# Loading chunks 1 to 3 of x from a second DMA queue in a transformer-block kernel

## The chip, the cores and the metric

The kernel runs on one core of a Trainium2 chip. The metric is the device time of one execution in microseconds (us), of the slowest core, which here is the only one. The kernel before takes 799.41 us (median of 3 runs, 799.39 to 799.5).

Engines carry their short names in the profile: PE is TensorE (PEld its weight loads), DVE is VectorE, ACT is ScalarE, POOL is GpSimd, SP is SyncE. SPq and ACTq are the sequencers of SyncE and ScalarE, which issue DMAs. Times in the views count from the start of the profiled span.

## The reference

A pre-norm block: a segmented attention with a memory, then a gated MLP, both with a residual. Only its first step matters here: the layer norm of x, 2048 rows of 1024 in bf16, and the projection of its first 512 rows.

```python
def _layernorm(x, axis=-1, eps=1e-05):
    m = jnp.mean(x, axis=axis, keepdims=True)
    v = jnp.var(x, axis=axis, keepdims=True)
    return (x - m) / jnp.sqrt(v + eps)

x = A_x
h = x + _A_ref(_layernorm(x, axis=-1), A_wq, A_wk, A_wv, A_wo, A_beta)   # attention, 4 segments of 512
h2 = h + _B_ref(_layernorm(h, axis=-1), B_w_in, B_w_sp, B_b_sp, B_w_out) # gated MLP
```

## The kernel before

A small recorder lists the operations of each engine in program order and puts in the semaphore waits. (So every operation has the same source line, L209, in the profile.) Each engine has its own instruction stream; SyncE does nothing but issue DMAs.

The first segment is four chunks of 128 rows of x, 256 KB each. They are loaded in turn with four 256 KB pieces of w_v, all by SyncE:

```python
def x_load(tc):
    sp.dma_start(XCH[tc % 4][:], x2d[tc * 128:(tc + 1) * 128, :])

for k in range(8):
    if k in (0, 1, 3, 5):
        x_load((k + 1) // 2)
    else:
        i = {2: 0, 4: 2, 6: 4, 7: 6}[k]
        sp.dma_start(WV[0][:, i:i + 2, :],
                     A_wv[i * 128:(i + 2) * 128, 0:512].rearrange("(c p) n -> p c n", p=128))
sp.dma_start(WK[:, :, 0:256], wcols(A_wk, 0, 256))
sp.dma_start(BETAB[:], A_beta.partition_broadcast(128))
# ... more weights ...
act.activation(RDM[:, 0, 0:1], MHALF[:], ACTF.Exp)   # ScalarE's first activation: brings its table load forward
```

The start of the computation. `warm` keeps TensorE busy while x is under way; `center` subtracts the mean (the division comes later, in the projections); `pe_Th` transposes a chunk on TensorE with eight 128-wide matmuls and copies the result out:

```python
warm(9)                                    # nine 512-wide matmuls on zeros
act_mean(1)                                # mean of chunk 1 on ScalarE
var0(ln_stats(XCH[0]))                     # mean and variance of chunk 0 on VectorE
c0 = center(0, MV[0][:, 0:1], ALU.subtract)
c1 = center(1, MEAN[1][:])
pe_Th(0, c0, dve, dve)
pe_Th(1, c1, act, dve)
act_mean(2)
rstd0(0)
var0(ln_stats(XCH[1]))
rstd0(1)
c2 = center(2, MEAN[2][:])
act_mean(3)
# ... first half of the w_v projection of chunks 0 and 1, then pe_Th(2, c2, act, dve) ...
```

The softmax here doesn't subtract the row's maximum and nothing guards it: scores larger than these inputs give would overflow.

Of the kernel before, what the change touches and what calls it, by code (L numbers as in the profile page):

```python
# [257 lines left out]
def bass_sequential_preLN__memory_aug_infini_attn__mixer_gmlp__prompt_kernel(  # L258
# [14 lines left out]
    x2d = A_x[0]  # L273
    out2d = out[0]
    R = _Recorder(nc)
    pe, act, dve, pool, sp = R.pe, R.act, R.dve, R.pool, R.sp
# [69 lines left out]
    XCH = [b2("xch%d" % i, [128, D], BF16) for i in range(4)]  # L346
# [43 lines left out]
            pe.matmul(dst, lhs(i), rhs(i), start=(i == 0), stop=(i == n - 1))  # L390


    def x_load(tc):
        sp.dma_start(XCH[tc % 4][:], x2d[tc * 128:(tc + 1) * 128, :])

    def wcols(ap, lo, hi):
        return ap[:, lo:hi].rearrange("(c p) n -> p c n", p=128)

    for k in range(8):
        if k in (0, 1, 3, 5):  # L400
            x_load((k + 1) // 2)
        else:
            i = {2: 0, 4: 2, 6: 4, 7: 6}[k]
            sp.dma_start(WV[0][:, i:i + 2, :],
                         A_wv[i * 128:(i + 2) * 128, 0:512].rearrange("(c p) n -> p c n", p=128))
# [318 lines left out]
    for tc in range(4, 8):  # L724
        x_load(tc)
# [44 lines left out]
    for n in range(LAST + 1):  # L770
# [30 lines left out]
        if s < NSEG - 2 and c >= 4:  # L801
            x_load(4 * (s + 2) + c - 4)
# [87 lines left out]
    for tb in range(4):  # L890
# [9 lines left out]
        for tcl in range(4):  # L900
            tc = 4 * tb + tcl
# [38 lines left out]
```

## Time and profile before

| | kernel before |
|---|---|
| time, median of 3 | 799.41 us |
| traced run | 799.35 us |
| TensorE busy | 790.4 of 797.3 us |
| chunk 0 asked for / landed | 0.80 / 3.54 us |
| first transpose starts | 5.80 us |
| transposes of chunk 2 start | 9.97 us |

The page of the kernel before, its busy times and the chain that ended last:

```profile
PE 790.4 (99%) x5657; PEld 378.9 (48%) x5657; DVE 377.3 (47%) x745; ACT 295.5 (37%) x347; POOL 170.6 (21%) x329
...
PE 96%; DVE 2%; ACT 1%; issue 0%; DMA 0%; DVEq 0%
```

TensorE is the limit. A change of the first DMAs can only matter where TensorE stands still for want of their data, which is in the first 10 us. There, the chain of waits of the kernel before, in order of time (start, length, what):

```profile
0.80 2.74 DMA xch<-in_A_x_dram
...
3.56 0.70 DVE stats L209
...
5.26 0.50 DVE lno L209
...
5.80 1.74 PE ps L209 x16
...
7.57 0.42 DVE xnT L209
...
9.57 0.36 DVE lno L209
...
9.97 13.08 PE ps L209 x80
```

Read it from below: the long run of TensorE that begins at 9.97 us waits for chunk 2 to be centred on VectorE. VectorE goes from one thing to the next since the statistics of chunk 0, with two short waits for the transposes (0.31 and 0.27 us), and the statistics wait for the DMA of chunk 0. That is the only DMA on the chain.

The timeline of the same run (start, length, engine, operation, tiles, count; in brackets the idle time before and what ended it):

```profile
0.79 1.28 ACT L209 ACT_TABLE_LOAD   x1 [0.79 <-PEq L925]
0.80 0.87 SPq L209 DMA_DIRECT2D xch<-in_A_x_dram  x2
...
4.25 1.06 ACT L209 ACTIVATE junk<-xch 128x1024 bf16<-128x1024 bf16 x1 [1.96 <-DMA xch<-in_A_x_dram]
...
5.80 1.73 PE L209 MATMUL ps<-ident,lno 128*128 128x128 bf16 x16 [0.18 <-DVE lno L209]
```

ScalarE does wait for chunk 1, but its mean is done before VectorE asks for it. The sixteen transposes take 1.73 us.

### The profile page before, as it was taken

Reading aid. Unit: us, or ns where it says so; the run is one execution under the profiler, and the core shown is the slowest. Engines: PE = TensorE matmul, PEld = TensorE weight load, DVE = VectorE, ACT = ScalarE, POOL = GpSimd, SP = SyncE. Lnnn points to the kernel's source line nnn. Section 1 sums busy time; section 2 is a strip of 40 time slices with the busy share of each in tenths; the row PEclk is TensorE's granted clock in tenths of the full one; section 3 lists DMA queues with packets and bytes.
Section 4 is the critical chain, followed back from the end, with each engine's and each line's share of the span. In section 5 each row is a group of like instructions: output and inputs, shape, how many; then the busy total and the mean of one; then the engine's idle time right before and its main releaser. Section 6 shows DMA issues by size and latency. Waiting matters only on the chain.

```text
span 797.3 us, 13127 instructions
## 1 busy us (share of the span) xinstructions
PE 790.4 (99%) x5657; PEld 378.9 (48%) x5657; DVE 377.3 (47%) x745; ACT 295.5 (37%) x347; POOL 170.6 (21%) x329
## 2 busy tenths in 40 slices
PE   8999999999999999999999999999999999999998
PEld 4444455554454455455544444444444444444444
DVE  6764688579844766744562000153233324323432
ACT  5777877787787675133333333100000000000000
POOL 4564565556553331100230000000000000000000
PEclk9999999999999999999999999999999999999999
DMA  9662555363414425411116000740270153021002
GB/s 299 172 166 53 94 81 121 87 107 93 95 27 122 113 65 135 125 47 53 53 54 132 1 1 1 223 87 7 82 129 1 34 122 63 1 67 46 1 8 85
DMA packets 125002, 64.83 MB, mean 81 GB/s; under 512 B 94992, under 2 KB 113936, under 8 KB 124944
## 3 DMA queue, kind: packets, MB, share of 16 engines
q1 hardware_dynamic: 124944, 63.99, 33.0%
q8 instruction: 44, 0.72, 0.4%
q14 instruction: 14, 0.11, 0.0%
HBM read 32.51 MB, written 8.39 MB: 51 GB/s over the span
## 4 chain that ended last, share of the span: by engine, by line
PE 96%; DVE 2%; ACT 1%; issue 0%; DMA 0%; DVEq 0%
PE ps L209 96%; DVE stats L209 1%; ACT e L209 0%; DVE lno L209 0%; DMA xch<-in_A_x_dram 0%; DVE hch L209 0%; DVE ta L209 0%; DVE otok L209 0%; ACT qk L209 0%; DVE rdm L209 0%; DVE mv L209 0%; DVE pqk L209 0%; DVE etmp L209 0%; DVE rd L209 0%; DVE upd L209 0%
## 5 line engine op out<-in xcount | busy, mean ns | idle before, releaser
L209 PE MATMUL ps<-wspT,z 128*128 128x512 bf16 x896 | 194.0, 379 | 0.0
L209 ACT ACTIVATE e<-ps 128x2048 bf16<-128x2048 f32 (+1 forms) x96 | 152.7, 1590 | 49.3 <-PE ps L209 49.2
L209 PEld LDWEIGHTS ps<-wspT,z 128*128 128x128 bf16 x896 | 87.7, 98 | 105.7
L209 DVE TENSOR_TENSOR tmpg<-ps,brow 128x512 f32<-128x512 f32 x56 | 38.7, 691 | 196.8 <-DMA brow<-in_B_b_sp_dram 103.5
L209 POOL TENSOR_SCALAR_AFFINE_SELECT e<-e 128x512 bf16<-128x512 bf16 x128 | 87.9, 699 | 129.5 <-ACT e L209 129.3
L209 PE MATMUL ps<-win,hnT 128*128 128x448 bf16 x512 | 98.3, 352 | 0.0
L209 PE MATMUL ps<-w_out,yT 128*128 128x512 bf16 (+2 forms) x462 | 97.4, 373 | 0.0
L209 PE MATMUL ps<-hnT,win 128*128 128x512 bf16 x448 | 96.9, 379 | 0.0
L209 PEld LDWEIGHTS ps<-win,hnT 128*128 128x128 bf16 x512 | 49.7, 98 | 46.4 <-issue 0.2
L209 PEld LDWEIGHTS ps<-w_out,yT 128*128 128x128 bf16 x462 | 44.7, 98 | 52.3
L209 PEld LDWEIGHTS ps<-hnT,win 128*128 128x128 bf16 x448 | 43.8, 98 | 52.8
L209 PE MATMUL ps<-xnT,wk 128*128 128x512 bf16 x256 | 60.8, 380 | 0.0
L209 PE MATMUL ps<-xnT,wq 128*128 128x512 bf16 x256 | 60.6, 379 | 0.0
L209 PE MATMUL ps<-wv,xnT 128*128 128x512 bf16 x256 | 59.4, 380 | 0.2 <-ACT xnT L209 0.2
L209 PE MATMUL ps<-wo,oT 128*128 128x512 bf16 x256 | 58.0, 379 | 0.9 <-DVE upd L209 0.9
L209 ACT ACTIVATE z<-ps 128x448 bf16<-128x448 f32 x60 | 32.5, 543 | 69.5 <-PE ps L209 69.5
L209 ACT ACTIVATE z1T<-ps 128x512 bf16<-128x512 f32 x56 | 33.4, 597 | 63.3 <-PE ps L209 63.3
L209 DVE TENSOR_TENSOR fin<-fin,ps 128x512 bf16<-128x512 bf16 (+2 forms) x33 | 22.2, 672 | 71.2 <-DMA fin<-out_dram 38.1
L209 DVE BATCH_NORM_STATS2 zst<-z 128x6 f32<-128x448 bf16 x64 | 38.9, 619 | 30.1 <-ACT z L209 30.1
L209 PEld LDWEIGHTS ps<-v,e 128*128 128x128 bf16 x1280 | 37.3, 96 | 9.1 <-issue 1.7
L209 DVE TENSOR_TENSOR yT<-tmpg,z1T 128x512 bf16<-128x512 f32 x56 | 38.7, 692 | 1.9
L209 PE MATMUL ps<-v,e 128*128 128x33 bf16 x1280 | 38.4, 177 | 0.0
(86 smaller groups left out, 608.4 us busy)
## 6 DMA issues: line engine op xcount, KB each, us to landing
xch<-in_A_x_dram SPq DMA_DIRECT2D x16, 256.0 KB, 3.0
xr<-in_A_x_dram SPq DMA_DIRECT2D x16, 256.0 KB, 3.8
out_dram<-hch SPq DMA_DIRECT2D x16, 256.0 KB, 2.4
fin<-out_dram SPq DMA_DIRECT2D x16, 256.0 KB, 2.7
out_dram<-fin SPq DMA_DIRECT2D x31, 128.0 KB, 1.7
win<-in_B_w_in_dram SPq DMA_DIRECT2D x4, 896.0 KB, 5.1
w_out<-in_B_w_out_dram SPq DMA_DIRECT2D x1, 3584.0 KB, 12.7
win<-in_B_w_in_dram SPq DMA_DIRECT2D x3, 1024.0 KB, 5.2
```

The costliest lines, as they stand in the source:

```text
L209: ins = getattr(e, op.name)(*op.args, **op.kw)
```

## The change

The intent: chunks 1 to 3 are issued by ScalarE, whose sequencer is idle at the start, while SyncE issues chunk 0 and the w_v pieces. An issue costs SyncE about 0.45 us, so everything is asked for earlier.

```diff
-    def x_load(tc):
-        sp.dma_start(XCH[tc % 4][:], x2d[tc * 128:(tc + 1) * 128, :])
+    def x_load(tc, eng=sp):
+        eng.dma_start(XCH[tc % 4][:], x2d[tc * 128:(tc + 1) * 128, :])
@@
     for k in range(8):
         if k in (0, 1, 3, 5):
-            x_load((k + 1) // 2)
+            x_load((k + 1) // 2, act if k else sp)
```

## The prediction

> **What bounds the kernel now.** The page's busy table has TensorE busy 790.4 of 797.3 us (99%); 96% of the chain that ended last is TensorE. Only the first 10 us hold TensorE idle time that DMA could touch. The chain in order of time there is: x chunk 0's DMA, 0.80 to 3.54 us; VectorE's statistics of chunk 0 (3.56 to 5.0), aggregate (0.22), centring (0.50); TensorE's sixteen 128-wide transposes of chunks 0 and 1 (5.80 to 7.54, mostly at half clock: the clock record turns full at 7.2 us); a VectorE copy (0.42); statistics of chunk 1 (1.3), aggregate, centring of chunk 2 (0.36); TensorE from 9.97 until 23 us. Chunk 0 is the only DMA on it.
>
> By the DMA view in narrow windows chunk 1 lands at about 4.2 us, chunk 2 at 7.0, chunk 3 at 8.5. ScalarE waits for chunk 1 (2.0 us, waits view), but its mean is ready at 5.40, before VectorE gets to centring chunk 1 (5.66, directly behind chunk 0's). Chunk 2's mean starts at 7.80 and chunk 3's at 8.97, directly behind ScalarE's earlier work. The w_v pieces land at 6.3, 7.8, 9.2, 9.9, before TensorE uses them (7.37 and later, no DMA wait).
>
> **What the change moves.** Three issues leave SyncE (0.43 to 0.50 us each in the timeline), so its later issues come up to 1.4 us sooner. ScalarE gets three issues in front of its table load (1.28 us) and first activation (0.20): at 0.45 us each it is ready at about 3.6 us, before chunk 1 lands. Order on TensorE, VectorE and GpSimd is unchanged; no bytes are added.
>
> **What it costs.** Chunk 1 is now issued at 0.8 us, beside chunk 0 instead of behind it. The Trainium skill ("DMA: Bandwidth & Descriptors", Queues, rings and completion order) says that each DMA engine takes turns between its queues packet by packet. In the packet records of before, chunk 0's 128 packets of 2 KB ran alone from 1.8 to 2.9 us: 57 in the first 0.75 us, with engines part idle, then 44 per 0.25 us. If the slow start doubles with two queues, 256 packets finish at about 3.3 us, so chunk 0 lands about 0.4 us later (estimate: 3.9 to 4.0 instead of 3.54; 0.7 later if nothing overlaps, 0 if chunk 0 keeps its lead). This goes straight into the chain. Some may come back, as more of the sixteen transposes then run after the clock turns full (107 against 56 ns each); the Trainium skill ("TensorE: Matmul & The Clock Gate", Part 1) calls the clock window free-running, so this can fall either way.
>
> What it gains: chunks 1 to 3 and w_v land up to 2 us sooner, but nothing on the chain waits for them. From 10 us on the DMA engines carry the same bytes at the same rate.
>
> **Predicted time:** 799.7 us (range 799.2 to 800.5): about 0.3 us slower. Chances: faster by over 2% 0.003, within 2% 0.994, slower by over 2% 0.003.
>
> **Right if:** chunk 0 lands at 3.8 to 4.2 us and chunk 1 no later than 4.2; the first transpose starts 0.2 to 0.6 us later than 5.80; TensorE's long stretch starts later than 9.97; everything after 25 us is only shifted.
>
> **Wrong if:** issues on ScalarE cost near 1 us each, so that chunk 1's mean comes late (up to 1 us slower); chunk 0 lands unchanged (no change); the longer gap after the warm-up matmuls delays the full clock by a window (1 to 2 us slower); or earlier DMA issues let the start run faster than I see (a few tenths faster).

## The result, and the profile after

The changed kernel takes 800.1 us (median of 4 runs: 799.52 to 800.6) against 799.44 (4 runs: 799.39 to 799.5). The ratio is 1.001, with a 95% interval of 0.9995 to 1.0025. (Ratios are the mean time of one kernel's fast runs over that of the other's of the same rounds, so not quite the ratio of the medians quoted.) With every chip, the changed kernel ran 14 times, mean 799.98 us, and the kernel before 31 times beside the others (the five runs of b0 below are left out), mean 799.16: 0.8 us slower. In the three sets in which both ran, the difference of the means is 0.63, 0.71 and 0.91 us; the same comparison of the kernel before with itself gave 0.24 (run b0 below), so the sign is clear and the size is good to a few tenths.

The chain of waits of the changed kernel (traced run: 799.68 us):

```profile
0.80 3.75 DMA xch<-in_A_x_dram
...
4.57 0.70 DVE stats L209
...
6.27 0.50 DVE lno L209
...
6.82 0.41 PE ps L209 x4
...
7.25 1.09 DVE xnT L209 x3
...
9.92 0.36 DVE lno L209
```

and its timeline:

```profile
0.79 1.43 ACTq L209 DMA_DIRECT2D xch<-in_A_x_dram  x3
0.80 0.40 SPq L209 DMA_DIRECT2D xch<-in_A_x_dram  x1
1.25 1.97 SPq L209 DMA_DIRECT2D wv<-in_A_wv_dram  x4
2.24 1.28 ACT L209 ACT_TABLE_LOAD   x1 [2.24 <-issue]
...
4.76 1.06 ACT L209 ACTIVATE junk<-xch 128x1024 bf16<-128x1024 bf16 x1 [1.02 <-DMA xch<-in_A_x_dram]
...
6.82 1.07 PE L209 MATMUL ps<-ident,lno 128*128 128x128 bf16 x16 [1.17 <-DVE lno L209]
...
10.32 0.62 PE L209 MATMUL ps<-ident,lno 128*128 128x128 bf16 x8 [0.29 <-DVE lno L209]
```

Three things are to be seen. Chunk 0 lands at 4.55 us instead of 3.54 although it is asked for at the same 0.80. Everything on VectorE moves by that 1.01 us, and so does the first transpose (6.82 against 5.80). And by the transposes of chunk 2 only 0.35 us of the delay are left (10.32 against 9.97), because the sixteen transposes took 1.07 us instead of 1.73. ScalarE's table load, 1.45 us later than before, costs nothing: ScalarE still waits 1.02 us for chunk 1 after it.

The transposes were shorter because of TensorE's clock. The trace's clock record says full from 5.40 us on in this run, before the transposes, and from 7.22 us on in the traced run of the kernel before, in the middle of them. The transposes show it too: in the kernel before they start 107 ns apart up to 7.2 us and 56 ns apart after it; in this run all but the first are 56 ns apart. The Trainium skill ("TensorE: Matmul & The Clock Gate", Part 1) says that the gate looks at a free-running window of about 3.4 us, so the moment can differ from run to run with nothing changed. The traces agree: in two traces of the kernel before it was 7.22 and 4.25 us. This is a coin that every run tosses, and it is why single pairs of runs mislead here.

Where chunk 0's time went can be read from the DMA view, cut to 1 to 2.75 us. First the kernel before (packets of each queue, MB, share of the 16 engines' time):

```profile
DMA packets 101, 0.21 MB, mean 118 GB/s; under 512 B 0, under 2 KB 0, under 8 KB 101
...
q1 hardware_dynamic: 101, 0.21, 46.6%
```

and the changed kernel, whose second queue, q10, is ScalarE's:

```profile
DMA packets 53, 0.11 MB, mean 62 GB/s; under 512 B 0, under 2 KB 0, under 8 KB 53
...
q1 hardware_dynamic: 31, 0.06, 15.3%
q10 hardware_dynamic: 22, 0.05, 7.6%
```

Chunk 0 is 128 packets of 2 KB. Before, 101 of them were on their way by 2.75 us; after the change 31, with 22 of chunk 1 between them. The packets of the two queues came mixed, which agrees with the Trainium skill ("DMA: Bandwidth & Descriptors", Queues, rings and completion order): each DMA engine takes turns between the queues that have work for it. But not even the sum of both reached the old number, and the 16 engines were busy for 23% of this time instead of 47%. So it was not bytes that chunk 0 waited for. The two requests also ended together: in the three traces of the changed kernel chunk 0 landed at 4.55, 4.43 and 4.77 us, and ScalarE started on chunk 1 at 4.76, 4.65 and 4.61.

### The profile page after: what moved, and what is told of

The parts are those of the page before. It is cut to its first block, busy times and chain, and to the rows that moved or that the text cites. A ratio compares the mean times of both kernels' runs of the same rounds, so it can differ in the third digit from the quotient of the medians.

```text
span 797.6 us, 13035 instructions
## 1 busy us (share of the span) xinstructions
PE 784.7 (98%) x5565; PEld 378.3 (47%) x5657; DVE 377.1 (47%) x745; ACT 295.5 (37%) x347; POOL 169.8 (21%) x329
## 4 chain that ended last, share of the span: by engine, by line
PE 95%; DVE 2%; issue 1%; ACT 1%; DMA 0%; DVEq 0%
PE ps L209 95%; DVE stats L209 1%; DMA xch<-in_A_x_dram 0%; ACT e L209 0%; DVE lno L209 0%; DVE hch L209 0%; DVE ta L209 0%; DVE otok L209 0%; ACT qk L209 0%; DVE xnT L209 0%; DVE rdm L209 0%; DVE mv L209 0%; DVE pqk L209 0%; DVE etmp L209 0%; DVE rd L209 0%
## 5 line engine op out<-in xcount | busy, mean ns | idle before, releaser
L209 PE MATMUL ps<-xnT,wq 128*128 128x512 bf16 x225 | 53.9, 379 | 1.8 <-issue 0.2
## 6 DMA issues: line engine op xcount, KB each, us to landing
w_out<-in_B_w_out_dram SPq DMA_DIRECT2D x1, 3584.0 KB, 12.8
```

Source lines behind the costliest of these rows:

```text
L209: ins = getattr(e, op.name)(*op.args, **op.kw)
```

## The experiments

Twelve runs were made (nine edited kernels, the changed kernel twice more and the kernel before once more), in three calls, each call on one chip with nine runs of the kernel before (means 799.12, 799.10 and 799.15 us). In each run the kernel was timed five times; all results were correct against the reference. Two theories were at stake at the beginning: that chunk 0's landing makes the time, with the turn of the clock as a second, random term; and the rival that the scatter or the loss comes from elsewhere (ScalarE's issues and its late table load, or later DMAs).

All columns of the summary but the last come from the one traced execution of each run; "rest" is the traced run's time minus the start of the transposes of chunk 2.

| run | chunk 0 landed, us | first transpose | clock full at | transposes of chunk 2 | traced run, us | rest, us | mean of 5 minus mean of before, us |
|---|---|---|---|---|---|---|---|
| before (first trace) | 3.54 | 5.80 | 7.22 | 9.97 | 799.35 | 789.38 | |
| b0 before again | 3.61 | 5.87 | 4.25 | 9.38 | 799.41 | 790.03 | +0.24 |
| changed kernel (first trace) | 4.55 | 6.82 | 5.40 | 10.32 | 799.68 | 789.36 | +0.63 (4 runs) |
| a1 changed again | 4.43 | 6.70 | 5.46 | 10.21 | 799.57 | 789.36 | +0.71 |
| c4 changed, third | 4.77 | 7.04 | 5.99 | 10.55 | 799.91 | 789.36 | +0.91 |
| a2 ScalarE issues after table load | 3.96 | 6.22 | 6.33 | 9.77 | 799.13 | 789.36 | +0.34 |
| a3 chunk 1 back on SyncE | 4.13 | 6.40 | 4.46 | 10.47 | 799.81 | 789.34 | +0.53 |
| a4 12 warm-up matmuls | 4.56 | 6.84 | 7.14 | 10.48 | 799.84 | 789.36 | +0.56 |
| b1 chunk 1 first, one queue | 4.21 | 6.48 | 11.06 | 11.33 | 800.70 | 789.37 | +0.78 |
| b2 beta on ScalarE's queue | 5.25 | 7.51 | 11.20 (see text) | 11.82 | 801.19 | 789.37 | +2.03 |
| b3 chunk 0 in halves | first half 3.12 | 5.43 | 5.29 | 9.86 | 799.28 | 789.42 | +0.62 |
| c1 beta second, one queue | 3.57 | 5.83 | 6.28 | 10.82 | 800.20 | 789.38 | +0.98 |
| c2 ScalarE's issue held back | 3.53 | 5.80 | 7.06 | 9.91 | 799.28 | 789.37 | +0.15 |
| c3 5 warm-up matmuls | 4.64 | 6.91 | 11.25 | 11.64 | 801.00 | 789.36 | +1.77 |

The column "rest" is the first finding. In 13 of 14 traces it is 789.34 to 789.42 us. Everything that these kernels differ in has happened by 12 us; from there on the same work takes the same time. Earlier landings of w_v and of chunks 2 and 3 are worth nothing later.

### a1_after_again and c4_after_third: the changed kernel again

No edit.

> The changed kernel once more. Both theories: chunk 0 lands at 4.4 to 4.7 us (3.54 before). Clock theory (the runs at 799.6 and those at 800.5 differ in when the TensorE clock turns full): the times fall again into two groups about 0.9 us apart, and the profiled run's group goes with the turn: at about 5.3 us near 799.6, at 7 us or later near 800.5. Rival (the groups come from when chunk 0 lands): the profiled run's landing differs by about 1 us between groups, with the turn playing no part. Mean over the runs 0.4 to 0.9 us above the kernel before.

> The changed kernel a third time, beside the others. Chunk 0 lands at 4.4 to 4.7 us again. Times in two groups near 799.6 and 800.6, about one run in three in the slow one; if the profiled run is of the slow group, the clock theory says that its clock turns full after 8 us.

Measured: 799.57, 800.79, 799.58, 799.56, 799.68 and 799.91, 800.6, 800.42, 799.71, 799.63 us. Chunk 0 landed at 4.43 and 4.77 us (the second a little past the stated 4.7), against 3.54 and 3.61 in the two traces of the kernel before. With the first four runs, 9 of 14 runs lie between 799.52 and 799.91 and 5 between 800.42 and 800.79. No traced run fell in the slow group, so the changed kernel itself does not show its cause; a4 and c3 below bear on it.

### b0_before_again: the kernel before again

No edit.

> The kernel before once more, for a second trace. Theory (two terms: chunk 0's landing and the moment at which the TensorE clock turns full): chunk 0 lands at 3.5 to 3.7 us again, and its times scatter from 798.4 to 800.4 with the turn: at a turn before 5.8 us, where the transposes start, 798.4 to 798.6; at a turn near 7.2 about 799.4; later more. Rival (the scatter comes from the DMA): the landing of chunk 0 moves by half a microsecond or more between this trace and the first one, in the direction of the time.

Measured: 799.41 (traced), 799.44, 799.08, 798.92, 799.82 us; the nine runs beside it 798.67 to 799.57. The landing came as expected, and so did the early clock with an early start of chunk 2's transposes (9.38 us). The time did not: it should have been 798.4 to 798.6. The trace shows where the gain of 0.59 us went. The waits view of this run between 26 and 38 us has a line that the first trace does not have:

```profile
PE ps L209 <- DMA pk<-pqk: 0.6, 1, 0.6
```

At 29.6 us TensorE stood 0.56 us for a DMA transpose. That transpose was asked for at 19.48 us and took 10.6 us to land; in the first trace it was asked for at 20.07 and took 8.3. The large w_k and w_q loads were in flight for most of that time and were slower as well: 10.6 and 14.2 us to land, against 9.1 and 12.8. Why they were slower in this run is not shown. So a start that is half a microsecond early can be lost again to this transpose. How often that happens in the kernel before is open: it was traced twice, and its runs reach down to 798.44.

### b1_x1_first: chunk 0 late, with ScalarE left alone

```diff
-            x_load((k + 1) // 2)
+            x_load({0: 1, 1: 0, 3: 2, 5: 3}[k])     # in the kernel before: chunk 1 ahead of chunk 0
```

> The kernel before with SyncE issuing chunk 1 ahead of chunk 0; ScalarE issues nothing. Theory (chunk 0's landing goes straight into the time, whatever queue delays it): chunk 0 lands near 4.2 us, 0.7 later than before, first transpose at 6.4 to 6.6, fastest runs at 799.0 to 799.3 against 798.44 before. Rival (ScalarE's issues or its delayed table load cost the time): equal to before.

Measured: 799.34, 799.39, 799.6, 800.37, 800.7 us; mean 0.78 above before, fastest run 0.67 above the fastest of before (798.67). The landing moved by 0.6 to 0.7 us (4.21), the first transpose as well. Chunk 0's landing goes into the time, and ScalarE's issues and late table load are not needed for it. As the whole cause this rival is out; for the changed kernel itself the table load is cleared by its trace, where ScalarE waits 1.02 us for chunk 1 after it.

The traced run was the slowest, and shows the slow group of this kernel. TensorE's lines of its timeline:

```profile
6.48 1.89 PE L209 MATMUL ps<-ident,lno 128*128 128x128 bf16 x16 [0.71 <-DVE lno L209]
8.15 3.34 PE L209 MATMUL ps<-wv,xnT 128*128 128x512 bf16 x8
```

The clock became full only at 11.06 us, so all sixteen transposes and the eight w_v matmuls (3.34 us; 1.68 for seven of them in the changed kernel's trace) ran at half speed.

### a4_warm12 and c3_warm5: the idle stretch and the clock

```diff
-    warm(9)
+    warm(12)      # a4; in c3: warm(5); both in the changed kernel
```

> The changed kernel with 12 instead of 9 warm-up matmuls, so that TensorE is busy to about 6.9 us, until the first transpose can start (6.8 us). Clock theory (the idle stretch from 5.6 to 6.8 us puts off the full clock in some runs): the slow group is gone, all runs 799.5 to 799.8. Rival (groups come from DMA landing): groups as in the plain changed kernel, 0.9 us apart.

> The changed kernel with 5 instead of 9 warm-up matmuls, so that TensorE is idle from about 3.9 to 6.8 us. Clock theory (the slow group are runs in which the idle stretch put off the full clock beyond the transposes): the clock turns full only after 9 us, transposes take 107 ns each, and every run is in the slow group or above it: 800.4 to 801.2. Rival (the groups have another cause): two groups at 799.6 and 800.6 as before.

Measured: a4 799.53 to 799.84 us, five runs, none slow. c3 800.54 to 801.55, five runs, all slow (one above the stated 801.2); its trace has the full clock at 11.25 us and 1.89 us for the sixteen transposes:

```profile
6.91 1.89 PE L209 MATMUL ps<-ident,lno 128*128 128x128 bf16 x16 [3.00 <-DVE lno L209]
```

So a longer idle stretch ahead of the transposes puts off the full clock, and by about 1 us of time. In the changed kernel that stretch is 1.17 us, against 0.18 in the kernel before (the brackets in the timelines above). That its slow third of runs comes from this is likely, not shown: a4's five fast runs would come up by chance about one time in nine ((9/14) to the fifth power), and no slow run of the changed kernel itself was traced. The clock records add support. In b2 (below) the clock turned in steps of 3.41 us, and in the other 13 traces the record's full stretch lasts 231 or 232 such steps (788.48 or 791.89 us). Counted back in such steps from the turn to full, TensorE was busy for 78% or more of the last step in all 14 traces, and for 79% or less of the steps before it in which the clock did not turn. A step that holds the whole idle stretch of 1.17 us is busy for at most 66%. An estimate from this: slide the steps over the first trace of the changed kernel, and about four placements in ten leave the full clock until after the transposes, none in the kernel before's first trace; 5 of the 14 runs were slow. The busy share is not the whole rule, though: b0 turned at 78%, while b1 with 79% had to wait for the next step.

### a2_act_late: ScalarE's issues behind its table load

```diff
-            x_load((k + 1) // 2, act if k else sp)
+            if k == 0:
+                x_load(0)
@@
     act.activation(RDM[:, 0, 0:1], MHALF[:], ACTF.Exp)
+    for tc in (1, 2, 3):
+        x_load(tc, act)
```

> Chunks 1 to 3 still on ScalarE's queue, but issued behind its table load and first activation (first issue at about 2.3 us). Sharing theory (chunk 0 is late because chunk 1 moves beside it): chunk 0 lands at 3.5 to 3.8 us as before, chunk 1 at 5.0 to 5.8 and its mean at 6.2 to 7.0, so the wait moves to chunk 1: 0.2 to 1.0 us slower than before, by another path. Rival (use of a second queue delays chunk 0 whenever it is): chunk 0 lands at 4.3 us or later.

Measured: 799.0 to 800.21 us, mean 0.34 above before. The edit did not do what it was meant to: ScalarE's sequencer did not wait for the table load or the activation. It issued chunk 1 at 0.93 us, while the table load ran from 0.79 to 2.07. But this accident is telling. The second request came 0.13 us after chunk 0's, and the packets up to 2.75 us were

```profile
q1 hardware_dynamic: 106, 0.21, 56.4%
q10 hardware_dynamic: 3, 0.01, 1.6%
```

Chunk 0 was on its way as in the kernel before (103 of the 106 packets are its data), and only its last 25 packets met those of chunk 1. The chain has its landing:

```profile
0.80 3.16 DMA xch<-in_A_x_dram
```

It landed at 3.96 us, by neither theory's number (3.5 to 3.8, or 4.3 and later).

### a3_x01_sp: chunk 1 back on SyncE

```diff
-            x_load((k + 1) // 2, act if k else sp)
+            if k < 2:
+                x_load(k)
@@
     act.activation(RDM[:, 0, 0:1], MHALF[:], ACTF.Exp)
+    for tc in (2, 3):
+        x_load(tc, act)
```

> Chunks 0 and 1 first on SyncE's queue as before, chunks 2 and 3 on ScalarE's behind its table load. Sharing theory: chunk 0 lands at 3.5 to 3.7 us, chunk 1 at 4.2 to 4.5, first transpose at 5.8 to 6.0 us, time equal to before within 0.2 us although chunks 2 and 3 and the w_v pieces land sooner: early landings of these are worth nothing. Rival (the earlier landings are worth something, masked by chunk 0 in the changed kernel): 0.3 us or more faster than before.

Measured: 799.51 to 799.87 us, mean 0.53 above before; expected was equal. ScalarE's issues again did not wait (0.93 us), so chunk 2 competed with chunks 0 and 1: chunk 0 landed at 4.13 us and chunk 1 at 5.64 (expected 4.2 to 4.5), and the chain went over chunk 1's mean. This run tells nothing for the question that it was made for, as the expectation rested on a late issue. It shows that chunk 1 must land in time as well: by about 4.5 us, an estimate from its mean, which takes 1.16 us on ScalarE in this run's chain, and from the 5.66 us at which VectorE turns to chunk 1 in the first trace. Later than that, the mean holds up VectorE.

### b2_tiny_on_act and c1_beta_second_sp: bytes, or two requests at once?

```diff
-    sp.dma_start(BETAB[:], A_beta.partition_broadcast(128))
+    # b2: act.dma_start(BETAB[:], A_beta.partition_broadcast(128)) as ScalarE's very first instruction
+    # c1: sp.dma_start(BETAB[:], A_beta.partition_broadcast(128)) right behind chunk 0
```

> The kernel before with only the 8 KB load of beta (128 rows of 64 bytes) moved to ScalarE's queue at the very start. If chunk 0 is late in the changed kernel because of the bytes of chunk 1: chunk 0 lands at 3.5 to 3.7 us here, time as before. If it is late because any second request at the same moment holds up the making of its packets: chunk 0 lands at 4.0 us or later, with a thin start of its packets (under 45 in the first 0.75 us against 57).

> The kernel before with the 8 KB load of beta as SyncE's second DMA, right behind chunk 0, nothing on ScalarE. If two queues asked at the same moment are what holds up chunk 0: chunk 0 lands at 3.5 to 3.8 us as before (5.25 with beta on ScalarE's queue), and only what stands behind beta, chunk 1, is late. Rival (the small rows slow whatever is in flight, from either queue): chunk 0 lands at 4.3 us or later.

Measured: b2 800.47 to 801.49 us, mean 2.03 above before. An 8 KB load, asked for on ScalarE's queue at the same moment, made chunk 0 land at 5.25 us, later than 256 KB there did. The two requests and the landing of chunk 0, and the packets up to 2.75 us, in b2:

```profile
0.79 0.40 ACTq L209 DMA_DIRECT2D betab<-in_A_beta_dram  x1
...
0.79 4.45 DMA xch<-in_A_x_dram
...
DMA packets 57, 0.04 MB, mean 24 GB/s; under 512 B 38, under 2 KB 38, under 8 KB 57
...
q1 hardware_dynamic: 19, 0.04, 13.2%
q10 hardware_dynamic: 38, 0.00, 1.1%
```

The engines were busy 14% of this time. So chunk 0 does not lose to the bytes of the other request, nor to engine time; here, too, the two went out side by side and ended together (beta landed at 5.1 us). In c1 the same 8 KB, second on SyncE's own queue, left chunk 0 alone (3.57 us), which speaks against small rows slowing whatever is in flight, and it was chunk 1 behind them that came late. But SyncE needs about 0.45 us for an issue, so beta was asked for at 1.25 us, and c2 below shows that such a head start is enough with a second queue too. Whether one queue would also serve two requests of the same moment side by side, no run shows. The chain of c1:

```profile
1.72 4.29 DMA xch<-in_A_x_dram
...
6.03 1.16 ACT junk L209 x2
```

It cost 0.98 us by way of chunk 1's mean. The load of beta is slow from either queue (2.8 us to land in c1, 4.3 in b2).

In b2 the long wait also cost the clock: full at 4.38 us, half again at 7.79 after 2.45 us without work for TensorE, full at 11.20, in steps of 3.41 us. This is the window length that the Trainium skill gives in "TensorE: Matmul & The Clock Gate", Part 1.

### c2_act_held: the change with ScalarE held back half a microsecond

```diff
     act.activation(RDM[:, 0, 0:1], MHALF[:], ACTF.Exp)
     pool.iota(IOT[:], [[1, 128]], base=0, channel_multiplier=-1)
+    pool.memset(XCH[1][:, 0:2], 0.0)      # chunk 1's DMA has to wait for this write
+    for tc in (1, 2, 3):
+        x_load(tc, act)
```

(The loop at the top loads chunk 0 alone from SyncE, as in a2.)

> Chunks 1 to 3 on ScalarE's queue behind its table load, with chunk 1 held back by a small GpSimd write into its buffer, so that it is asked for at about 1.3 to 1.5 us, half a microsecond after chunk 0. Theory (only a request at the same moment takes turns with chunk 0 from its first packet on): chunk 0 lands at 3.5 to 3.8 us, chunk 1 by 4.6, third copy of the transposed chunks no later than in the kernel before at the same turn of the clock; times within 0.3 us of before. Rival (any use of the second queue delays chunk 0): 3.95 us or later.

Measured: 798.96, 799.15, 799.28, 799.46, 799.66 us, mean 0.15 above before, less than the kernel before differed from itself. The requests of ScalarE, and what VectorE waited for:

```profile
1.24 0.96 ACTq L209 DMA_DIRECT2D xch<-in_A_x_dram  x2
...
3.55 1.43 DVE L209 BATCH_NORM_STATS2 stats<-xch 128x6 f32<-128x512 bf16 x2 [1.83 <-DMA xch<-in_A_x_dram]
...
6.15 0.49 DVE L209 TENSOR_SCALAR lno<-xch,mean 128x1024 bf16<-128x1024 bf16 x1 [0.41 <-ACT junk L209]
```

Up to 2.75 us the only queue with packets was

```profile
q1 hardware_dynamic: 97, 0.20, 40.8%
```

and chunk 0 landed at 3.53 us. Chunk 1 landed a little late (ScalarE started on it at 4.97 us; expected by 4.6). VectorE then waited 0.41 us for its mean; in this trace the clock turned at 7.06 us, and the transposes at half speed hid that. Three x chunks on the second queue do not delay chunk 0 when they are asked for 0.44 us after it. They brought no gain, and no loss that five runs can tell from the scatter.

### b3_x0_halves: less to wait for?

```diff
-            x_load((k + 1) // 2)
+            if k == 0:
+                for lo in (0, 512):
+                    sp.dma_start(XCH[0][:, lo:lo + 512], x2d[0:128, lo:lo + 512])
+            else:
+                x_load((k + 1) // 2)
```

> The kernel before with chunk 0 loaded as two DMAs of 512 columns each on SyncE's queue, so that VectorE's first statistics wait for half the bytes. Theory (chunk 0's landing is what the start waits for): first half lands 0.2 to 0.5 us before 3.54, second half by 4.0, fastest runs 0.1 to 0.4 us below those of before. If 1 KB packets or the extra issue (0.45 us) eat it: equal, or up to 0.3 us slower.

Measured: 799.28 to 800.4 us, mean 0.62 above before, beyond the worst that was expected. VectorE did start 0.42 us earlier (3.14), but chunk 1, now third in the queue, landed at 5.04 us instead of 4.2 and its mean became the wait, as in a3 and c1.

No version beat the kernel before.

## Why the prediction was right, and which step of it failed

- **The limit and the chain: right.** Chunk 0's DMA was the one DMA on the chain, and its delay moved every step up to the first transpose by the same 1.0 us. b1 shows it without ScalarE.
- **The sign: right.** Predicted 799.7 us with a range of 799.2 to 800.5; measured 800.1. Over all runs the change cost 0.8 us, where about 0.3 had been predicted. The range also holds the time of the kernel before (799.44), so landing in it proves little. And that the traced run's 799.68 us meets 799.7 so well is luck: a delay that was put 0.6 us too small was offset by 0.66 us that the clock gave back in that run.
- **"If the slow start doubles with two queues ... chunk 0 lands about 0.4 us later": this is the step that failed.** The term measured 1.0 us (0.8 to 1.2 over the three traces against the two of before). Two queues did not double the thin start; they thinned it: 33, 53 and 74 packets from both queues by 2.75 us in the three traces of the changed kernel, against 101 and 94 from the one queue before. The prediction's outer bound, 0.7 us "if nothing overlaps", was too small for the same reason: it took the total rate as given. Chunk 1, expected by 4.2 us, was late as well: ScalarE started on it at 4.76.
- **"The first transpose starts 0.2 to 0.6 us later": wrong, 1.02,** for that reason.
- **"Some may come back" through the clock: right.** In the traced run 0.66 of 1.01 us came back, as transposes at full clock. The reverse case, named under what would make it wrong ("the longer gap after the warm-up matmuls delays the full clock by a window"), is what b1 and c3 show in their slow runs; for the changed kernel's slow third of runs it is likely.
- **"Issues on ScalarE cost near 1 us each": no.** Three took 1.43 us together, and the later table load was hidden.
- **"Nothing on the chain waits for" the earlier landings: right.** The rest of the kernel takes 789.34 to 789.42 us in all traces but one.

What stays open is why two requests at the same moment start so thinly. The engines were idle for most of the time and the packets missing, and the two requests ended together. A guess is that something both queues share, ahead of the engines, makes their packets; no run here shows it.

## What to carry to other kernels

A second DMA queue did not speed up the start of this kernel: when something else, even 8 KB, was asked for on it at the same moment (within 0.01 us), the load that everything waits for was 0.8 to 1.7 us late. Give the critical load a head start (here 0.44 us was enough and 0.13 us was not quite), and first ask whether anyone on the chain waits for the loads that you hurry. When effects are below 1 us, compare traces by a late, common milestone and compare the means of many runs: TensorE's clock alone moves a run by about as much.

## What the Trainium skill lacked or had wrong

- "DMA: Bandwidth & Descriptors", Issuing engines are not separate DMA queues: it says that issuing from several engines only saves issue time. Here it cost: chunk 0 landed at 4.43 to 4.77 us instead of 3.54 to 3.61, and both queues together started 33 to 74 packets by 2.75 us, one queue alone 94 or 101.
- The same page, Queues, rings and completion order: the turns by packet are there, but not that a small request can hold up a large one in step. An 8 KB load of 64-byte rows moved the landing of 256 KB from 3.54 to 5.25 us, with the engines 14% busy up to 2.75 us.
- "TensorE: Matmul & The Clock Gate", Part 1: the warm-up is told as about 3.4 us of time from the first work on. In the 14 traces TensorE's work began at 1.60 to 1.78 us and the full clock came between 4.25 and 11.25 us. The page does not say how much idle time inside a window puts it off. An idle stretch of 3.00 us ahead of the transposes (c3) or of 0.71 us (b1, one trace) went with a full clock after 11 us, one of 0.45 us (a2) did not; nor did 1.17 to 1.27 us in traces of the changed kernel, where the clock had turned by 5.99 us.
